# A Fourier-mixing and channel-mixing kernel: in the first batch, a butterfly two steps further down VectorE's queue, two PSUM evacuations exchanged between engines, and fewer filler products

## The chip, the cores and the metric

The kernel runs on one core of a Trainium2 chip. The metric is the time of one execution on the device, in microseconds (us). Times given for a kernel are medians of several runs; a profile is one further look at a single execution, and its span is the time from that execution's first recorded instruction to its last.

## The reference

For `x` of shape (8, 3072, 256) the kernel computes the real part of a two-dimensional Fourier transform of each batch, and then a channel mix with a look at the row before:

```python
X = fft(fft(x, axis=1), axis=2).real
X_prev = rows of X shifted down by one, first row zero
xk = mu_k * X + (1 - mu_k) * X_prev
xr = mu_r * X + (1 - mu_r) * X_prev
k  = relu(xk @ w_k)            # 256 -> 1024
v  = (k * k) @ w_v             # 1024 -> 256
out = sigmoid(xr @ w_r) * v
```

## The kernel before

**Tiling.** The transform over 3072 rows is split as 48 x 64. Per batch it goes through three product stages on TensorE (PE), each followed by a copy out of PSUM (an *evacuation*):

- Stage A (`a_sum`, L384, and `a_item`, L372) transforms over the 48. Batch 0 and the first half of batch 1 use `a_sum`, which takes `x` as it was loaded and does the sum over the two halves of the columns inside PE with two products per row group. The others use `a_item`, which takes sums and differences made beforehand on VectorE (DVE) by `butterfly` (L115). A butterfly `(b, h, e)` reads the loaded half `h` of batch `b` and makes the sum (`e` = 0) or the difference (`e` = 1).
- Stage B (`d_item`, L407) transforms over the 256 columns and writes `g_all`.
- Stage C (`c_item`, L418) transforms over the 64; its evacuation writes the tile `pq`. The arguments are a first slice and a number of slices of 64 columns.

From `pq`, DVE makes the spectrum and the mixed inputs: `halves` (L438), `diff` (L445), and `mix` or `mix2` (L479, L483), which run `scaled` (L453) and `mixed` (L466) and write the tiles `x00` to `x11`.

**The channel mix** works on 48 chunks of 512 rows, 6 per batch (two mirrored sets m of three). Each chunk has four pieces. `k_piece` (L502) does four products of 512 columns on PE and a relu on ScalarE (ACT). `square` (L511) squares two pieces on DVE. `r_item` (L515) does eight products of 256 columns, once per chunk, and a sigmoid on ACT. `v_tile` (L527) does eight products of 256 columns, and `v_out` (L538) multiplies two v tiles by the sigmoid on DVE and stores them.

**What sets the order.** The order is written out by hand and pinned per engine (`pin_order`, L85): each engine does its instructions in the order in which the program emits them. The main loop (L688) goes through 192 steps and 5 more. In step s it emits `k_piece` s, then the items of kind "x" that are due in s (stages A, B, C and `r_item`, in the order in which `at` was called), then `v_tile` of step s - 5, then the items of kind "w" (all DVE work and the loads of x), then, when s - 5 is odd, `v_out`, and in odd steps `square`. `at(step, function, ...)` (L596) enters an item; the lines that matter here are L609 to L660. An evacuation belongs to its stage's item, so it is emitted with the "x" items, on ACT unless the item's last argument is "V", which puts it on DVE (`evac`, L363).

**Buffers.** Product groups of the k and r products and of the stages A, B and C write to PSUM tiles `psW`, of which there are three, used in turn (`ps_w`, L74). So a group can begin only when the group three places before it has been evacuated. The v products and the fillers use `psV`, two in turn. There are two buffers for the loaded halves of x (`xh`, L109), so the load of half `(2, 1)` waits until the butterflies of `(1, 1)` have read it.

**Ahead of the loop** the first two stage C groups of batch 0 are done, DVE makes the first 512 columns of `x00`, and the first k products are split in two halves of 256 columns. `keep_busy(n)` (L138) emits n products of 512 columns of zeros that nobody reads: fillers for TensorE.

The steps that the change touches belong to the first batch. There `r_item` of the third chunk is due in step 12; it reads `x10`, whose last third is written by `mix2(0, 1, 0, 16, 24)`, due in step 10. `a_sum(1, 0, 4)` and `a_sum(1, 0, 8)` are due in step 5, `c_item(0, 17, 8)` in step 3.

Of the kernel before, what the change touches and what calls it, by code (L numbers as in the profile page):

```python
# [35 lines left out]
def kernel(  # L36
# [40 lines left out]
    def ps_v():  # L77
        return ps_slot("V", 2, 512)
# [34 lines left out]
    V = nc.vector  # L113
# [24 lines left out]
    def keep_busy(n):  # L138

        ps = ps_v()  # L140
        for _ in range(n):
            nc.tensor.matmul(out=ps[:, 0:512], lhsT=zeros[:, 0:P], rhs=zeros, start=True, stop=True)
# [346 lines left out]
    def k_products(c, ds, lo=0, hi=512):  # L489
        b, m, i = c  # L490
        xk = x_t[b, 0, m]
        if lo == 0:
            st["k", ds] = ps_w()
        for hs in range(2):
            fc = 2 * ds + hs
            for a in range(2):
                nc.tensor.matmul(out=st["k", ds][:, 512 * hs + lo:512 * hs + hi],  # L497
                                 lhsT=wk_sb[m][a][:, 128 * fc:128 * fc + 128],
                                 rhs=xk[:, a, 512 * i + lo:512 * i + hi],
                                 start=(a == 0), stop=(a == 1))  # L500
# [95 lines left out]
    def at(step, f, *args):  # L596
        work.setdefault((step, "x" if f in (a_item, a_sum, d_item, c_item, r_item) else "w"),
                        []).append((f, args))
# [10 lines left out]
    keep_busy(4)  # L609
    k_products(chunks[0], 0, 0, 256)  # L610
    k_products(chunks[0], 1, 0, 256)
    keep_busy(4)
    for n, c in enumerate(chunks):
        at(4 * n + 4, r_item, c)


    at(0, m_swap, NS1, NSL)
# [6 lines left out]
    at(1, mix2, 0, 0, 0, 8, 16)  # L624
    at(2, d_item, 0, 5)
    at(2, a_sum, 1, 0, 0)
    at(3, c_item, 0, 17, 8)
    at(3, butterfly, 1, 1, 0)
    at(4, halves, 0, 17, 25)
    at(4, diff, 0, 16, 24)  # L630
    at(5, a_sum, 1, 0, 4)
    at(5, a_sum, 1, 0, 8, "V")
    at(5, mix2, 0, 0, 0, 16, 24)
    at(6, a_sum, 1, 0, 12)
    at(6, c_item, 0, 25, 2)
    at(6, load_xh, 2, 0)
    at(6, mix2, 0, 1, 0, 8, 16)
    at(6, butterfly, 1, 1, 1)
    at(7, halves, 0, 25, 27)
    at(7, diff, 0, 24, 26)  # L640
    at(7, mirrored_mu)
# [92 lines left out]
```

## Time and profile before

| | us |
|---|---|
| median of 5 runs | 466.0 |
| lowest and highest of the 5 | 464.26, 466.8 |
| the profiled execution, its own time | 464.91 |
| its span | 463.1 |
| PE busy in the span | 452.6 (98%) |
| DVE busy | 357.6 (77%) |
| ACT busy | 357.6 (77%) |
| GpSimd busy | 34.9 (8%) |

The time of an execution is a little longer than its span: 464.91 beside 463.1.

How to read the lines. A line of a timeline gives the start in us from the beginning of the span, the duration of the merged instructions, the engine (PE for products, PEld for weight loads, DVE, ACT, POOL for GpSimd), the line of the kernel, the operation, the tile written and the tile read, the shape, how many instructions were merged (x8), and in brackets how long the engine sat idle before it and what ended the wait. Durations of successive instructions overlap by a little, so the distance between starts says how long an engine is really held. The ends of products are modelled, so for PE too the starts are what counts. A line of the chain that ended last gives start, length and what; it is followed back from the last instruction of the kernel, at each point to what released it.

The profile by stages (busy time of each engine between two moments) reads: from 24 to 32 us PE 7.27, DVE 7.09, ACT 7.86 of 8; from 32 to 52 us PE 19.46, DVE 19.51, ACT 15.79 of 20; from 52 to 456 us PE 404.00, DVE 310.06, ACT 319.52 of 404. The batches overlap: while the channel mix of one batch runs, the stages of the next are woven in.

### The profile page before, as it was taken

The page shows a single profiled execution, that of the slowest core. Times are in us where ns is not written, and L with a number is a line of the kernel's source. Part 1 is how long each engine was busy: PE and PEld are TensorE (multiplying, and loading weights), DVE is VectorE, ACT ScalarE, POOL GpSimd, SP SyncE. Part 2 cuts the span into 40 slices and gives each one's busy share as a digit, 9 for nine tenths or more (in the row PEclk, how much of TensorE's full clock was granted, in tenths as well). Part 3 has the DMA queues.
Part 4 walks back from the last instruction along what each step waited for, and adds up shares of the span by engine and source line. Part 5 has one row for each costly group of instructions (what it writes and reads, how often), then busy time and mean ns, then how long its engine had stood idle before and what let it go on. Part 6 is the DMA issues. An engine that isn't in the chain of part 4 may idle for free.

```text
span 463.1 us, 10098 instructions
## 1 busy us (share of the span) xinstructions
PE 452.6 (98%) x4266; PEld 332.3 (72%) x4266; DVE 357.6 (77%) x495; ACT 357.6 (77%) x390; POOL 34.9 (8%) x67
## 2 busy tenths in 40 slices
PE   6899999999999999999999999999999999999996
PEld 3667777777777777777777777777777777776665
DVE  7799968986788777978588776888679854898443
ACT  3897898788778887888778888878877888666662
POOL 8821000001000000000000000000000000000000
PEclk9999999999999999999999999999999999999999
DMA  7896451625612373224722265212222222223323
GB/s 120 146 169 106 113 126 47 138 68 115 137 47 70 58 146 95 69 58 92 156 63 62 54 137 115 69 47 69 49 68 55 60 65 51 70 53 80 74 64 96
DMA packets 32721, 40.24 MB, mean 87 GB/s; under 512 B 4228, under 2 KB 30340, under 8 KB 31332
## 3 DMA queue, kind: packets, MB, share of 16 engines
q1 hardware_dynamic: 27828, 25.05, 21.7%
q0 software_dynamic: 4688, 14.42, 18.4%
q8 instruction: 33, 0.54, 0.5%
q10 hardware_dynamic: 160, 0.13, 0.1%
q14 instruction: 12, 0.10, 0.1%
HBM read 28.84 MB, written 25.17 MB: 117 GB/s over the span
## 4 chain that ended last, share of the span: by engine, by line
PE 87%; DMA 4%; DVE 4%; POOL 2%; issue 1%; SPq 0%; POOLq 0%; DVEq 0%
PE psV L534 34%; PE psW L497 33%; PE psW L520 9%; PE psW L403 4%; DMA xh<-in_x_dram 4%; PE psW L430 4%; PE psW L379 4%; POOL xh L106 1%; DVE k L513 1%; DVE x L475 1%; DVE t L462 1%; DMA out_dram<-o 1%; DVE eo L119 1%; DVE o L543 1%; POOL mu_f L325 0%
## 5 line engine op out<-in xcount | busy, mean ns | idle before, releaser
L507 ACT ACTIVATE rl<-psW 128x1024 f16<-128x1024 f32 x192 | 196.7, 1025 | 87.6 <-PE psW L497 87.6
L497 PE MATMUL psW<-x,wk 128*128 128x512 f16 (+1 forms) x776 | 197.4, 377 | 1.3 <-DVE x L475 1.1
L534 PE MATMUL psV<-wv_sb,k 128*128 128x256 f16 x1536 | 198.6, 272 | 0.0
L513 DVE TENSOR_TENSOR k<-rl 128x2048 f16<-128x2048 f16 x96 | 117.4, 1223 | 65.0 <-ACT rl L507 64.3
L534 PEld LDWEIGHTS <-k 128*128 128x128 f16 x1536 | 143.6, 98 | 20.3
L497 PEld LDWEIGHTS <-wk 128*128 128x128 f16 x776 | 75.7, 98 | 51.7 <-issue 2.2
L543 DVE SCALAR_TENSOR_TENSOR o<-psV,r 128x512 f32<-128x512 f32 (+1 forms) x97 | 66.2, 683 | 29.0 <-PE psV L534 27.0
L475 DVE TENSOR_TENSOR x<-y,t 128x1536 f16<-128x1536 f16 (+2 forms) x74 | 62.9, 851 | 2.5
L367 ACT ACTIVATE a<-psW 128x768 f16<-128x768 f32 x61 | 49.2, 809 | 4.5 <-PE psW L393 4.4
L520 PE MATMUL psW<-wr,x 128*128 128x256 f16 x384 | 49.9, 273 | 0.4 <-DVE x L475 0.4
L525 ACT ACTIVATE r<-psW 128x1024 f16<-128x1024 f32 x48 | 49.0, 1021 | 1.3 <-PE psW L520 1.3
L520 PEld LDWEIGHTS <-x 128*128 128x128 f16 x384 | 37.5, 98 | 15.2 <-DVE x L475 1.0
L367 ACT ACTIVATE g_all<-psW 128x1024 f16<-128x1024 f32 (+1 forms) x47 | 47.7, 1021 | 0.0
L106 POOL DMA_DIRECT2D xh<-in_x_dram x38 | 19.7, 524 | 241.4 <-DVE eo L119 230.2
L403 PEld LDWEIGHTS <-a 128*128 128x128 f16 x384 | 25.0, 98 | 10.5 <-issue 0.4
L119 DVE TENSOR_TENSOR eo<-xh 96x2048 f16<-96x2048 f16 x26 | 31.6, 1214 | 0.6 <-DMA xh<-in_x_dram 0.6
L379 PEld LDWEIGHTS <-eo 96*128 96x128 f16 x416 | 23.4, 97 | 11.6
L367 ACT ACTIVATE pq<-psW 128x896 f16<-128x896 f32 (+5 forms) x33 | 28.6, 869 | 0.3 <-PE psW L430 0.3
L403 PE MATMUL psW<-w_eo,a 128*128 128x128 f16 x376 | 28.3, 219 | 0.3 <-ACT pq L367 0.3
L430 PEld LDWEIGHTS <-g_all 128*128 128x128 f16 x648 | 23.3, 98 | 6.9 <-ACT g_all L367 0.2
L379 PE MATMUL psW<-w_pm,eo 96*128 96x96 f16 x416 | 26.3, 206 | 0.0
L430 PE MATMUL psW<-m,g_all 128*128 128x64 f16 x648 | 24.5, 193 | 0.1
(89 smaller groups left out, 148.3 us busy)
## 6 DMA issues: line engine op xcount, KB each, us to landing
out_dram<-o SPq DMA_DIRECT2D x190, 128.0 KB, 2.4
xh<-in_x_dram POOLq DMA_DIRECT2D x28, 384.0 KB, 6.2
xh<-in_x_dram POOLq DMA_DIRECT2D x6, 192.0 KB, 6.2
wv_sb<-in_moe_w_v_dram POOLq DMA_DIRECT2D x1, 512.0 KB, 8.6
xh<-in_x_dram POOLq DMA_DIRECT2D x4, 96.0 KB, 7.2
out_dram<-o ACTq DMA_DIRECT2D x2, 64.0 KB, 2.0
out_dram<-o SPq DMA_DIRECT2D x2, 64.0 KB, 2.0
wk<-in_moe_w_k_dram,row_i POOLq DMA_INDIRECT x4, 4.8
```

What stands on the lines that cost most here:

```text
L367: nc.scalar.activation(out=out_ap, in_=in_ap, func=AF.Copy)
L379: nc.tensor.matmul(out=ps[:, 128 * i:128 * i + 96], lhsT=eo[:, 8 * j + i, e, :], rhs=w_pm[0:96, 0], start=True, stop=True)
L403: nc.tensor.matmul(out=_v(ps, 256 * i + 64 * (1 - e), [(128, 2), (1, 64)]), lhsT=a_t[b][:, e, 2 * u:2 * u + 2, :], rhs=w_eo[:, e, :], star ...
L430: nc.tensor.matmul(out=ps[:, o + 64 * i:o + 64 * i + 64], lhsT=g_all[:, u, col:col + 128], rhs=m[:, sl], start=first, stop=last)
L475: V.tensor_tensor(out=dst, in0=_v(y_t[b], 64 * (NSL * a + lo + 3 * m), [(1, n)]), in1=_v(x_t["t", a], 64 * lo, [(1, n)]), op=ALU.subtract ...
L497: nc.tensor.matmul(out=st["k", ds][:, 512 * hs + lo:512 * hs + hi], lhsT=wk_sb[m][a][:, 128 * fc:128 * fc + 128], rhs=xk[:, a, 512 * i + l ...
L507: nc.scalar.activation(out=st["rl"][:, 2 * ds:2 * ds + 2], in_=st["k", ds].rearrange("p (f t) -> p f t", f=2), func=AF.Relu, bias=0.0, sca ...
L513: V.tensor_tensor(out=k2_t[c][:, 2 * ds - 2:2 * ds + 2], in0=r, in1=r, op=ALU.mult)
L520: nc.tensor.matmul(out=ps[:, 256 * tb:256 * tb + 256], lhsT=x_t[b, 1, m][:, a, 512 * i + 128 * tb: 512 * i + 128 * tb + 128], rhs=wr_sb[m] ...
L525: nc.scalar.activation(out=st["r", c], in_=ps, func=AF.Sigmoid)
L534: nc.tensor.matmul(out=st["v"][:, 256 * h:256 * h + 256], lhsT=k2_t[c][:, fc, 128 * tb:128 * tb + 128], rhs=wv_sb[:, fc], start=(fc == 0), ...
L543: V.scalar_tensor_tensor(out=o.rearrange("p a b -> p (a b)")[:, 0:256 * n], in0=st["v"][:, 0:256 * n], scalar=16.0, in1=st["r", c][:, 256 ...
```

## The change

All of it lies in the first batch:

- The second group of fillers in front of the loop has 2 products in place of 4.
- `r_item` of the third chunk is due in step 13 in place of 12.
- The evacuation of `c_item(0, 17, 8)` (stage C, step 3) goes to DVE. That of `a_sum(1, 0, 8)` (stage A, step 5) goes from DVE to ACT.
- The butterfly `(1, 1, 0)` is due in step 5 in place of 3. In step 5 it is the first "w" item, since the call of `at` stands where it stood, ahead of `mix2(0, 0, 0, 16, 24)`.
- The butterfly `(1, 1, 1)` is due in step 7 in place of 6, ahead of `halves(0, 25, 27)`.

```diff
@@ -609,9 +609,9 @@
     keep_busy(4)
     k_products(chunks[0], 0, 0, 256)
     k_products(chunks[0], 1, 0, 256)
-    keep_busy(4)
+    keep_busy(2)
     for n, c in enumerate(chunks):
-        at(4 * n + 4, r_item, c)
+        at(4 * n + (5 if n == 2 else 4), r_item, c)
 
 
     at(0, m_swap, NS1, NSL)
@@ -624,18 +624,18 @@
     at(1, mix2, 0, 0, 0, 8, 16)
     at(2, d_item, 0, 5)
     at(2, a_sum, 1, 0, 0)
-    at(3, c_item, 0, 17, 8)
-    at(3, butterfly, 1, 1, 0)
+    at(3, c_item, 0, 17, 8, "V")
+    at(5, butterfly, 1, 1, 0)
     at(4, halves, 0, 17, 25)
     at(4, diff, 0, 16, 24)
     at(5, a_sum, 1, 0, 4)
-    at(5, a_sum, 1, 0, 8, "V")
+    at(5, a_sum, 1, 0, 8)
     at(5, mix2, 0, 0, 0, 16, 24)
     at(6, a_sum, 1, 0, 12)
     at(6, c_item, 0, 25, 2)
     at(6, load_xh, 2, 0)
     at(6, mix2, 0, 1, 0, 8, 16)
-    at(6, butterfly, 1, 1, 1)
+    at(7, butterfly, 1, 1, 1)
     at(7, halves, 0, 25, 27)
     at(7, diff, 0, 24, 26)
     at(7, mirrored_mu)
```

## The prediction, made before the changed kernel had run

> **What bounds the kernel now.** I read three views in this order. First the busy time by stages: from 52 us to 456 us TensorE (PE) is busy in all 404.00 of 404 us, so nothing that happens there can be shortened by reordering; whatever this change is worth must be a PE gap before 52 us. Only the start of the main loop is open.
>
> Second, the chain that ended last (start, length, what). It shows whom PE waits for last:
>
> ```profile
> 21.61 10.41 DMA xh<-in_x_dram
> ...
> 32.11 1.22 DVE eo L119
> 33.33 1.14 DVE k L513
> ...
> 50.35 0.44 DVE x L475
> 50.79 0.05 issue
> 50.84 0.94 PE psW L520 x7
> 51.78 0.45 PE psW L403 x8
> ```
>
> A load of x (second half of batch 1) lands at 32.02; VectorE (DVE) had stood still for it and starts the butterfly at 32.11. From there DVE works without a gap to 50.79, and there PE takes over. So a late landing at 32 us is paid once, at 50.84, by the first r product group that needs DVE's last mix.
>
> Third, the PE timeline around that point and around the fillers:
>
> ```profile
> 22.29 1.03 PE L142 MATMUL psV<-zeros 128*128 128x512 f16 x4
> 23.16 0.27 PE L497 MATMUL psW<-x,wk 128*128 128x256 f16 x1
> 23.61 0.93 PE L497 MATMUL psW<-x,wk 128*128 128x256 f16 x7 [0.18 <-DVE x L475]
> ...
> 49.20 1.03 PE L497 MATMUL psW<-x,wk 128*128 128x512 f16 x4
> 50.11 0.28 PE L520 MATMUL psW<-wr,x 128*128 128x256 f16 x1
> 50.84 0.94 PE L520 MATMUL psW<-wr,x 128*128 128x256 f16 x7 [0.44 <-DVE x L475]
> 51.61 0.61 PE L403 MATMUL psW<-w_eo,a 128*128 128x128 f16 x8
> ```
>
> One r product starts at 50.11 and the next only at 50.84. Eight of them take 0.87 us elsewhere (0.109 each), so PE lost 50.84 - 50.22 = **0.62 us**. Between 30.5 and 50.1 the starts of groups follow one another at their own lengths, except at step 5.
>
> Step 5 is ruled by ScalarE (ACT), which has no gap from 24.14 to 35.7:
>
> ```profile
> 31.17 1.11 ACT L367 ACTIVATE pq<-psW 128x1024 f16<-128x1024 f32 x1
> 32.07 1.12 ACT L507 ACTIVATE rl<-psW 128x1024 f16<-128x1024 f32 x1
> 32.98 1.14 ACT L525 ACTIVATE r<-psW 128x1024 f16<-128x1024 f32 x1
> ```
>
> There are three psW slots, used in turn, so a PE group waits until the group three places earlier has been emptied. The second of the two a_sum groups of step 5 waits for the sigmoid that ends at 34.12: the two groups take 33.25 to 34.82 = 1.57 us, where one alone (36.56 to 37.22) takes 0.66, so 0.25 us are lost. Waits of 0.04 to 0.05 stand before k5, k4's successor r and the first a_sum.
>
> **The change, part by part.**
>
> *r products of the third chunk, step 12 to 13.* PE then does in step 12: k products 0.87, stage B 0.45 (8 products), v 0.87; in step 13: k 0.87 and only then r. Counted from 49.20 (later 49.30, see below), r starts at 52.40. DVE's last mix ends at 50.79 now, about 50.34 then. Slack 2 us: the 0.62 us go. What is late next? ACT gets four copies in step 13 (relu, sigmoid, two of stage B) at a pitch of 0.92, 3.7 us, against 3.5 us of PE. I followed the slots: the tightest is the first stage C group of batch 1 in step 14, whose slot comes free at 56.41 where PE arrives at 56.40; all others have 0.1 to 0.6 us. The v_out that multiplies by this sigmoid is in step 14 at 59.48 on DVE, 5 us after it. So **-0.62**; bounds -0.62 and -0.3 (three waits of 0.1 by the ACT pitch).
>
> *Exchange of evacuations.* Stage C's copy of 128x1024 leaves ACT (0.90 of pitch at 31.17) for DVE. No DVE copy of that size is in the trace; the three that are, 384, 512 and 768 columns, take 0.557, 0.69 and 0.954, that is 1.03 ns a column, so 1024 would take 0.954 + 0.265 = 1.22 us, and hold DVE 1.14 (a copy's successor starts 0.08 before its end). Nearest rows as bounds: ACT's 1.07 for the same shape and DVE's 1.36 for 128x1152 int32. I take 1.22. In front of it on DVE is the square that starts at 30.32 and holds DVE until 31.46. So the slot comes free at 31.46 + 1.22 = 32.68 where ACT frees it at 32.28: the k products of step 5 start at 32.73 in place of 32.33, **+0.40**. On the other hand ACT now does relu 4 and the sigmoid earlier (the sigmoid ends near 33.6, since it follows its products, done at 32.45), so the 0.25 wait and one of 0.05 vanish: k5 32.73, a_sum 33.60 and 34.26, v at 34.92 where it is 34.82 now. Net **+0.10**. Bounds: -0.34, if the copy frees its slot by 32.29 (0.25 + 0.05 + 0.04), and +0.25 with the 1.36 row. The a_sum copy that goes from DVE (0.87 of occupancy) to ACT (0.69) follows the relu that ends at 34.8 and is done by 36.3; its slot is wanted at 37.3. ACT has 1.03 us idle there now, so it costs nothing; without that cover it would be 0.69.
>
> *Butterflies down the queue.* The first, 1.14 of occupancy, goes from step 3 to step 5, behind the square, halves and diff; the second from step 6 to 7, behind one v_out. DVE's sum from 31.54: -0.57 idle, -0.87, +1.14, with the overlaps about -0.45; everything from step 5 on is that much earlier. Consumers of the butterflies: stage A of step 7, PE at 39.2, the result there at 36.4 (now 33.3); step 9, PE at 44.3, the result at 42.1. Behind them: the squares that v needs are earlier, not later. The load into the buffer that the second butterfly frees is issued on GpSimd at 42.4 in place of 42.18; it is read by DVE after 57. So **0** on the path in this execution. But the landing may now slip to about 35.1 before any engine waits, where now every 0.1 us of slip is 0.1 us at 50.84.
>
> *Two fillers less.* 4 x 0.216 become 2 x 0.216: PE is free at 22.72 in place of 23.16. The half-group behind needs DVE's x, whose two parts end at 23.03 and 23.56. So the first product starts 0.08 earlier, and the other seven again at 23.61: **0**. Cover: the wait for DVE. What it can cost is the clock. At the start eleven fillers take 4.87 us, 0.443 each, twice the 0.216 of later: PE begins at half rate. Between 20.14 and 23.61 PE now idles 0.51 + 0.77 + 0.34 = 1.62 of 3.47 us, then 2.06, but the longest single gap stays 0.77, and the unbroken gap from 9.07 to 10.52 left the next 16 products at the same 1.48 us as those before it. So I take 0; the other end is in the rival below.
> [...]
>
> **Sum.** -0.62 + 0.10 = -0.52 us on the profiled execution: 464.91 becomes 464.4 (span 463.1 to 462.6, 1.8 outside it). The median of the five runs is 466.0, 1.09 above the profiled one. If that excess arises before 21 us, the change leaves it: 465.5. If it is a later landing of x at 32 us, which DVE hands on to PE in full, it goes: 464.4. The trace has one execution and can't tell; I take the middle, **464.9 us**, with 464.4 to 465.5 around it.
>
> **Rivals.**
> 1. *More is won.* The excess is all due to the landing, and the stage C copy on DVE is as quick as its lower bound: -0.62 - 0.34 = -0.96, 463.95 on the profiled execution, say 463.9. For it: the one load on the chain of waits is this one, in flight for 10.4 us while the DMA engines are full. Against: the extrapolated 1.22.
> 2. *The wait moves, and nothing is won.* The copy takes 1.36 (+0.25) and ACT makes PE wait in steps 13 and 14 (0.3 of the 0.62 given back): -0.07, 465.9 from the median. For it: a slot with no margin at 56.4. Against: ACT has the same pitch there as now.
> 3. *Slower: the clock falls* near 23.5 because PE is idle 59% of 3.47 us where it was 47%. The only half-rate stretch in the trace is 4.87 us long. Such a stretch does half its work, 2.43 us lost, of which the PE gaps between 23.6 and 28.5 (0.16 + 0.47 + 0.46 = 1.09) absorb at most 1.09. With -0.62 for r that is +0.7 to +1.8: 466.7 to 467.8, middle 467.3. It decides as soon as a stretch of over 3.5 us (1.09 + 0.62, doubled) is at half rate. Against: the 1.45 us gap that did nothing.
>
> **How the numbers follow.** Forecast 0.55, rival 1 0.18, rival 2 0.15, rival 3 0.12. A measurement of this kernel can tell about 0.3% (1.4 us) from no change; the bounds are 464.6 and 467.4. The forecast's own range lies on both sides of 464.6: 0.20 faster, 0.35 same. Rival 1 is faster (0.18), rival 2 same (0.15), rival 3 slower 0.10 and same 0.02. So faster 0.38, same 0.52, slower 0.10. The range goes from below rival 1 to the mild end of rival 3: 463.5 to 466.7.
>
> **What would show it.** Right: no gap inside the r products of the third chunk, which stand behind k of step 13; DVE without idle time at 31.5 and the butterfly at about 35.1; the stage C copy at 31.46 for 1.2 us; k of step 5 at 32.7 and v at 34.9; products of 256 columns at 0.109 from 23.6 on; PE without gaps from 36 us on. Wrong: group times near double after 23.6 (the clock), a copy well off 1.2, waits on ACT between 53 and 57, or the same 0.6 us in front of another group in steps 12 to 16. If the span falls by 0.5 and the median by as little, the excess was not the landing.

## The result, and the profile after

| | before | after |
|---|---|---|
| median, us (64 and 38 runs) | 465.23 | 464.31 |
| lowest, highest | 464.16, 467.42 | 462.98, 465.88 |
| profiled execution, own time and span | 464.91, 463.1 | 464.33, 462.6 |

The ratio of the times is 0.9975, with a 95% interval of 0.9968 to 0.9982: the changed kernel is 0.25% (1.16 us, 0.84 to 1.49) faster. That is a gain, and smaller than 0.3%. The two profiled executions differ by 0.58 us. The spread differs too. Of the 64 runs before, 41 took over 465 us, of the 38 after only 3. Of the runs after, 14 are under the lowest of before, and 18 lie between 464.20 and 464.45.

The PE timeline of the changed kernel, around the fillers and at the r products of the third chunk:

```profile
22.22 0.59 PE L142 MATMUL psV<-zeros 128*128 128x512 f16 x2
23.02 0.27 PE L497 MATMUL psW<-x,wk 128*128 128x256 f16 x1 [0.20 <-DVE x L475]
23.55 0.92 PE L497 MATMUL psW<-x,wk 128*128 128x256 f16 x7 [0.26 <-DVE x L475]
...
49.23 1.03 PE L497 MATMUL psW<-x,wk 128*128 128x512 f16 x4
50.09 0.61 PE L403 MATMUL psW<-w_eo,a 128*128 128x128 f16 x8
50.53 1.04 PE L534 MATMUL psV<-wv_sb,k 128*128 128x256 f16 x8
51.41 1.03 PE L497 MATMUL psW<-x,wk 128*128 128x512 f16 x4
52.27 1.04 PE L520 MATMUL psW<-wr,x 128*128 128x256 f16 x8
53.15 1.06 PE L403 MATMUL psW<-w_eo,a 128*128 128x128 f16 x16
```

The eight r products now stand as one group of 0.88 us between starts; the hole of 0.62 us is gone. At the fillers PE waits a little longer for DVE and goes on at the same place (23.55 beside 23.61).

DVE in the kernel before, where it waits for the load, then in the changed kernel, and PE at step 5 of the changed kernel:

```profile
32.11 1.22 DVE L119 TENSOR_TENSOR eo<-xh 96x2048 f16<-96x2048 f16 x1 [0.57 <-DMA xh<-in_x_dram]
```

```profile
31.39 1.22 DVE L365 CAST pq<-psW 128x1024 f16<-128x1024 f32 x1
32.53 1.21 DVE L513 TENSOR_TENSOR k<-rl 128x2048 f16<-128x2048 f16 x1
...
35.05 1.21 DVE L119 TENSOR_TENSOR eo<-xh 96x2048 f16<-96x2048 f16 x1
```

```profile
32.66 1.02 PE L497 MATMUL psW<-x,wk 128*128 128x512 f16 x4 [0.28 <-DVE pq L365]
33.52 1.49 PE L393 MATMUL psW<-w_pm,xh 96*128 96x192 f16 x16
34.84 1.04 PE L534 MATMUL psV<-wv_sb,k 128*128 128x256 f16 x8
```

DVE has no idle time for the load any more; the stage C copy took 1.22 us. The k products of step 5 wait for that copy, the a_sum pair after them takes 1.32 in place of 1.57, and v comes at 34.84, where it came at 34.82. The chain that ended last now goes from DVE to PE at that copy, at 32.66, and not at the r products at 50.84.

### The profile page after: what moved, and what is told of

Same layout as the page of the kernel before. It is cut to its first block, busy times and chain, and to the rows that moved or that the text cites. A ratio compares the mean times of both kernels' runs of the same rounds, so it can differ in the third digit from the quotient of the medians.

```text
span 462.6 us, 10095 instructions
## 1 busy us (share of the span) xinstructions
PE 451.2 (98%) x4264; PEld 332.0 (72%) x4264; DVE 358.0 (77%) x495; ACT 357.6 (77%) x390; POOL 35.1 (8%) x67
## 4 chain that ended last, share of the span: by engine, by line
PE 92%; DVE 3%; DMA 2%; POOL 1%; issue 0%; ACT 0%; SPq 0%; POOLq 0%; DVEq 0%
PE psV L534 36%; PE psW L497 35%; PE psW L520 9%; PE psW L403 4%; PE psW L379 4%; PE psW L430 4%; DMA xh<-in_x_dram 2%; POOL xh L106 1%; DVE t L462 1%; DVE x L475 1%; DMA out_dram<-o 1%; PE psW L393 0%; DVE y L442 0%; DVE d L450 0%; DVE pq L365 0%
## 5 line engine op out<-in xcount | busy, mean ns | idle before, releaser
L367 ACT ACTIVATE pq<-psW 128x896 f16<-128x896 f32 (+5 forms) x32 | 27.4, 861 | 0.3 <-PE psW L430 0.3
```

Source lines behind the costliest of these rows:

```text
L367: nc.scalar.activation(out=out_ap, in_=in_ap, func=AF.Copy)
```

## The experiments

Theories, as they stood after this profile. **L**, the landing: the load of x (1, 1) lands near 32 us, at a somewhat different time in each execution; DVE waits for it and PE waits for DVE at the r products, so the kernel before pays each lateness in full. **R** and **Q**: what was taken away is the wait of the r products, a matter of queue order, and the spread of the runs comes from the start. **X**: the gain is the lighter queue of ACT. **F**: fillers are paid in executions in which PE comes late.

The kernels ran in three groups of four; each group has its own runs of the kernel before, and ratios are against those.

| kernel | median, us | before in its group | ratio (95%) | span of its profile |
|---|---|---|---|---|
| late_before | 467.93 | 466.67 | 1.0021 (1.0007 to 1.0035) | 466.4 |
| late_after | 466.00 | 466.67 | 0.9978 (0.9964 to 0.9992) | 464.2 |
| early_before | 467.26 | 466.67 | 1.0008 (0.9996 to 1.0020) | 465.3 |
| r_only | 466.92 | 466.67 | 1.0004 (0.9996 to 1.0013) | 465.2 |
| no_r | 464.53 | 465.70 | 0.9982 (0.9968 to 0.9997) | 461.8 |
| no_x | 464.32 | 465.70 | 0.9967 (0.9952 to 0.9982) | 461.4 |
| fill4 | 464.35 | 465.70 | 0.9971 (0.9958 to 0.9984) | 462.5 |
| no_bf | 464.36 | 465.70 | 0.9973 (0.9960 to 0.9986) | 462.4 |
| r_only_2 | 466.73 | 466.74 | 0.9996 (0.9985 to 1.0007) | 465.6 |
| x_only | 466.83 | 466.74 | 0.9999 (0.9987 to 1.0010) | 464.8 |
| bf_only | 468.24 | 466.74 | 1.0034 (1.0019 to 1.0049) | 466.4 |
| split | 466.77 | 466.74 | 0.9997 (0.9986 to 1.0008) | 465.7 |

In the first and the third group the kernel before itself is 1.0 us above the second. The kernel before was not profiled in these groups, nor was the whole change without a further edit among their kernels. Every profile there shows a late start with the same kind of wait, told under the first group. The profiled executions with a halved clock in their middle (late_before, early_before, r_only, r_only_2, bf_only, split) have a mean granted clock of 0.991 to 0.996, the others 0.998 to 1.000; the runs are compared on that below.

### The load later or earlier

late_before is the kernel before, late_after the changed kernel, both with:

```diff
         nc.gpsimd.dma_start(out=wv_sb, in_=moe_w_v.rearrange("(fc p) v -> p fc v", p=128))
-        load_xh(1, 1)
         for a in range(2):
             gather(wk_sb[1][a], moe_w_k, 2 + a)
+        load_xh(1, 1)
```

> The kernel before, with the load of x (1, 1) issued behind the two gathers of the second w_k, about 2.6 us later. Theory L (the gain is the landing of this load, which DVE hands on to the r products): DVE waits longer ahead of the butterfly of step 3, by as much as the landing is later, some 1 to 2 us from its 32.0; the butterfly and the square behind it start later by that, and the v products of step 5 or the r products of the third chunk wait longer by the same; time 1 to 2 us above the kernel before, 466.2 to 467.2. Theory Q (the gain is the order of r and the lighter ACT queue; the spread of the runs arises elsewhere): at most 0.3 us slower, 465.5.

> The changed kernel with the same later load. Theory L: the landing stays ahead of 35.05, where DVE now comes to the butterfly, so no wait of DVE for a load and the time of the changed kernel, 464.3 (0.2% under the kernel before). Theory Q: the same as for the kernel before with the later load, that is 0 to 0.3 us above the changed kernel. If the landing falls behind 35.05, slower by the difference.

early_before is the kernel before with:

```diff
+        load_xh(1, 1)
         nc.gpsimd.dma_start(out=wv_sb, in_=moe_w_v.rearrange("(fc p) v -> p fc v", p=128))
-        load_xh(1, 1)
```

> The kernel before, with the load of x (1, 1) issued ahead of that of w_v, about 1 us earlier. Theory L: DVE's wait of 0.57 us at 31.5 goes, and with it most of the 0.62 us ahead of the r products of the third chunk (0.05 to 0.15 stay); the runs lie closer together; 464.3 to 464.6, nearly the whole gain of the change with none of its edits. Theory Q: the r products wait as before, 465.2.

The signs came as L has them for the later load: 0.21% slower before, no loss after. For the earlier load L failed: nearly the whole gain was expected, and the ratio is 1.0008. But the profiles don't let either count as proof. DVE in late_before, then in early_before:

```profile
35.06 1.21 DVE L119 TENSOR_TENSOR eo<-xh 96x2048 f16<-96x2048 f16 x1
```

```profile
32.79 1.22 DVE L119 TENSOR_TENSOR eo<-xh 96x2048 f16<-96x2048 f16 x1
```

In neither does DVE wait for the load: it comes to the butterfly at 35.06 and 32.79, because everything before had become late. The last line of the load's semaphore events is at 34.2 in late_before and 34.7 in late_after, 2.2 and 2.6 us later than the 32.02 of the kernel before, and still ahead of DVE. So the expected cost could not appear in these executions. The halved clock, told next, adds to the times of some runs but does not explain the order: among the runs with a mean granted clock of 0.998 or more, six of late_before have a median of 467.53, eleven of the kernel before 466.46 and eleven of late_after 465.99. That fits L: the later load costs the kernel before about 1 us and leaves the changed kernel ahead; but no such run of late_before was profiled, and what it waits for is not shown.

In late_before, r_only, early_before, r_only_2, bf_only and split TensorE's granted clock is 0.50 for one or two stretches of 3.41 us. The stages of r_only_2 around one of them, and one stage of x_only (of the same group, without a halving):

```profile
core 0: us, PE busy (x) PEld busy (x) DVE busy (x) ACT busy (x) POOL busy (x), PEclk, DMA share, GB/s
26.75:30.16 3.41, 1.54 (x19) 1.07 (x17) 1.52 (x5) 2.25 (x4) 0.75 (x1) 1.00 1.07 208
30.16:33.57 3.41, 3.40 (x21) 2.24 (x21) 3.31 (x7) 2.71 (x4) 0.00 (x0) 0.50 1.06 192
```

```profile
26.36:29.77 3.41, 1.81 (x20) 1.23 (x19) 1.50 (x5) 2.23 (x3) 1.09 (x1) 1.00 1.10 210
29.77:33.18 3.41, 3.00 (x41) 1.98 (x39) 3.27 (x7) 3.41 (x5) 0.00 (x0) 1.00 1.04 188
```

In r_only_2 PE was busy for 1.54 of 3.41 us, and in the next 3.41 us the clock was 0.50; in x_only it was busy for 1.81, and the clock stayed 1.00. All eight halvings in these profiles, leaving out those behind the last products, follow a stretch with 1.15 to 1.61 us of PE (34 to 47%). In no_r a stretch has 1.75 (4.54 to 7.95, 51%) and none follows: the mean clock of that execution is 1.000. The longest single wait does not sort them: it is 1.49 us in split's stretch, which was followed by a halving, and 1.60 us in x_only's, which was not.

What emptied those stretches is a wait of 1.5 to 2.6 us that has no work behind it, PE in r_only_2:

```profile
27.07 0.61 PE L403 MATMUL psW<-w_eo,a 128*128 128x128 f16 x8
29.25 0.61 PE L403 MATMUL psW<-w_eo,a 128*128 128x128 f16 x8 [1.57 <-ACT pq L367]
30.17 1.44 PE L393 MATMUL psW<-w_pm,xh 96*128 96x192 f16 x8 [0.31 <-ACT rl L507]
```

PE waits for ACT's copy, and ACT is idle too, waiting for PE, whose groups are recorded as done: in early_before the stage C group starts at 23.98 and the last group ahead of the wait at 25.51 (0.61 long); ACT's copy of the stage C group begins at 27.62, after 2.39 us without work, and PE goes on at 28.70, after 2.57. Similar waits of PE, of 2.45, 2.08 and 2.38 us, stand between 14 and 18 us in late_before, r_only and bf_only. The first halving in late_before and bf_only, at 7.4 us, is another case; it follows a wait of 2.0 us for DVE at the start of stage A. What held the copies back is not shown. What the waits do is: PE comes to the k products of step 3 at 32.80 in late_before, where it is 28.89 in the kernel before, and DVE to the butterfly at 35.06 for 31.54, when the load has landed.

### Single parts

r_only and r_only_2 are the same kernel: the kernel before with

```diff
-        at(4 * n + 4, r_item, c)
+        at(4 * n + (5 if n == 2 else 4), r_item, c)
```

> The kernel before with one edit: the r products of the third chunk in step 13. Both theories: the wait of 0.62 us goes, since DVE's last mix ends near 50.8 and the products start near 52.3; no new wait between 52 and 57. Theory L: a landing up to 1.5 us later is covered too, unless the v products of step 5 meet the square late (their margin is 0.35 us), so most of the excess goes: 464.3 to 464.6. Theory Q: only the wait goes, 464.6, and the spread of the runs stays that of the kernel before.

> The kernel before with the r products of the third chunk in step 13 alone, once more, beside the other single parts. Theory L (the landing near 32 to 32.7 us, handed on by DVE, is what the kernel before is paced by; any edit that keeps DVE's lateness from PE brings the gain): the wait ahead of r goes, the slack behind it is 1.5 us; the v products of step 5 meet the square late only if the landing is behind 32.6. Ratio 0.9975 to 0.9985 on a chip where the first run of this kernel's long idle times of ACT between 14 and 28 us don't occur. Rival: the single edit brings nothing (ratio 1.000, as in the first run), since PE then waits for the square in step 5 instead.

x_only is the kernel before with `"V"` added to `c_item(0, 17, 8)` and taken from `a_sum(1, 0, 8)`:

```diff
-    at(3, c_item, 0, 17, 8)
+    at(3, c_item, 0, 17, 8, "V")
...
-    at(5, a_sum, 1, 0, 8, "V")
+    at(5, a_sum, 1, 0, 8)
```

> The kernel before with the two evacuations exchanged and nothing else. Theory L: DVE does the stage C copy while the load is still under way, comes to the butterfly at 32.5, and is 0.45 us earlier from there on when the landing is before that; of the 0.62 us ahead of the r products of the third chunk 0.15 to 0.2 stay; the k products of step 5 wait 0.4 for DVE, the second a_sum no longer for the sigmoid. Ratio 0.9985 to 0.999. Theory X (ACT's queue): 0.998.

bf_only is the kernel before with the butterflies alone:

```diff
-    at(3, butterfly, 1, 1, 0)
+    at(5, butterfly, 1, 1, 0)
...
-    at(6, butterfly, 1, 1, 1)
+    at(7, butterfly, 1, 1, 1)
```

> The kernel before with the two butterflies in steps 5 and 7 and nothing else. No wait of DVE for the load; but DVE stands idle for about 1 us ahead of the a_sum copy of step 5, which PE finishes at 35.0, and the butterfly comes behind that. DVE's last mix ends 0.2 to 0.3 us later than in the profile of the kernel before, and the wait ahead of r grows from 0.62 to about 0.9. Theory L: ratio 1.000, between 0.999 and 1.0005: what the landing no longer costs, the hole costs. Theory that the butterfly's place alone is the gain: 0.998.

Neither r alone nor the exchange alone gained anything (1.0004, 0.9996, 0.9999). But these runs are of the groups with the late start; DVE waits for the load in none of the profiles, so L has nothing to win there. Nor has R: late_before and early_before have r of the third chunk in step 12, and their eight r products already run in one piece (53.98 to 54.86 and 52.90 to 53.77). What the single edits do in an undisturbed execution is not shown. In r_only_2 there is no hole at the r products either. In x_only there is one, 52.10 to 52.53:

```profile
52.10 0.27 PE L520 MATMUL psW<-wr,x 128*128 128x256 f16 x1
52.53 0.94 PE L520 MATMUL psW<-wr,x 128*128 128x256 f16 x7
```

With 0.109 for the first product it is 0.32 us, more than the 0.15 to 0.2 expected. bf_only is clearly slower, 0.34%, and more than expected; its profile has the hole of DVE and what it costs at the r products:

```profile
37.88 0.96 DVE L365 CAST a<-psW 128x768 f16<-128x768 f32 x1 [1.00 <-PE psW L393]
```

```profile
52.14 1.03 PE L497 MATMUL psW<-x,wk 128*128 128x512 f16 x4
53.38 0.28 PE L520 MATMUL psW<-wr,x 128*128 128x256 f16 x1 [0.21 <-DVE x L475]
54.10 0.94 PE L520 MATMUL psW<-wr,x 128*128 128x256 f16 x7 [0.44 <-DVE x L475]
```

From 52.14 + 0.87 = 53.01 the first product waits 0.37 us and the second 0.61, together 0.98; 0.9 was expected. That is about two thirds of the 1.5 us by which the median is longer; the profile also has two halved stretches, and only three of its eleven runs have a mean clock of 0.998 or more (median 467.72, the kernel before 466.58), so the rest is not sorted out. The butterflies' move alone is a loss, as far as this group can tell: it needs the exchange to fill DVE's time, or r out of its way, as in no_r and no_x below.

### The change without one of its parts

Each is the changed kernel with one part as before: no_r has r of the third chunk in step 12, no_x the evacuations on their old engines, no_bf the butterflies in steps 3 and 6, fill4 four fillers (the diffs above, read backwards; for fill4 `keep_busy(2)` is `keep_busy(4)`).

> The changed kernel with the r products of the third chunk back in step 12. Theory R (the wait ahead of them is what the change took away): in an execution without other delays PE reaches them at 50.1 and DVE's last mix ends at 50.35, so 0.1 to 0.3 us of the wait come back; 0.05% above the changed kernel, ratio to the kernel before 0.998. Theory L (the landing): the butterfly is out of the way of the landing already, so the same 0.998. If ACT's queue counts (theory X), as good as the changed kernel.

> The changed kernel with the two evacuations on their old engines (stage C on ACT, the a_sum of step 5 on DVE). Theories R and L: the k products of step 5 no longer wait for DVE (0.44 us), but the second a_sum of step 5 waits for the sigmoid (0.25), and DVE stands idle for about 1 us until that a_sum is done; PE comes to the v products of step 5 at 34.8 as before; same time as the changed kernel, ratio 0.9975. Theory X (the gain lies in the lighter ACT queue): 0.4 to 0.9 us above the changed kernel, ratio 0.9985 to 0.9995.

> The changed kernel with four fillers in the second group, as before. Theories R, L and X: the same time as the changed kernel, ratio 0.9975, since the k products wait for DVE either way. Theory F (in executions where PE comes late to this place, x is there already and every filler is paid): up to 0.43 us above the changed kernel, ratio 0.998 to 0.9985; on the other hand no execution in which the clock halves near 23.5.

> The changed kernel with the two butterflies back in steps 3 and 6; stage C's copy on DVE stays ahead of the first. Theory L: the butterfly starts at 32.5 behind that copy, so a landing up to 0.5 us later than 32.0 is covered and a later one is passed on to DVE only, while the r products of step 13 keep 1.5 us of slack: same time as the changed kernel when the landing is before 33, ratio 0.9975; if landings are often later, the square behind it comes late for the v products of step 5 and the time rises by 0.3 us or more. Theories R, X, F: ratio 0.9975.

All four are as fast as the whole change (0.9975, measured against other runs of the kernel before) within what this group can tell (0.9967 to 0.9982, intervals of 0.0013 to 0.0015 to each side). So no single part is needed for a gain, and X falls: without the exchange the ratio is 0.9967. F is not seen: with four fillers 0.9971, though the interval reaches the 0.998 that F would give. Nor is the gain a matter of the clock: among the runs with a mean granted clock of 0.998 or more, 28 of the kernel before have a median of 465.51, and no_r, no_x, fill4 and no_bf have 464.52, 464.32, 464.35 and 464.36.

The profiles say why. no_r keeps a small rest of the hole; its r group takes 50.27 - 49.19 = 1.08 us between starts, 0.21 more than 0.87, where 0.1 to 0.3 was expected:

```profile
49.19 1.25 PE L520 MATMUL psW<-wr,x 128*128 128x256 f16 x8
50.27 0.61 PE L403 MATMUL psW<-w_eo,a 128*128 128x128 f16 x8
```

no_x has the expected hole on DVE ahead of the a_sum copy, and its butterfly after it:

```profile
33.86 0.96 DVE L365 CAST a<-psW 128x768 f16<-128x768 f32 x1 [0.91 <-PE psW L393]
34.73 1.21 DVE L119 TENSOR_TENSOR eo<-xh 96x2048 f16<-96x2048 f16 x1
```

It costs nothing, since r is in step 13 and has the slack. no_bf is the one that shows the landing, DVE and then PE:

```profile
30.08 1.22 DVE L365 CAST pq<-psW 128x1024 f16<-128x1024 f32 x1
32.68 1.22 DVE L119 TENSOR_TENSOR eo<-xh 96x2048 f16<-96x2048 f16 x1 [1.39 <-DMA xh<-in_x_dram]
33.83 1.22 DVE L513 TENSOR_TENSOR k<-rl 128x2048 f16<-128x2048 f16 x1
```

```profile
33.53 0.60 PE L534 MATMUL psV<-wv_sb,k 128*128 128x256 f16 x4
35.10 0.61 PE L534 MATMUL psV<-wv_sb,k 128*128 128x256 f16 x4 [0.96 <-DVE k L513]
```

This execution started 1.3 us quicker than that of the changed kernel (its v products would have run on from 33.53, where the changed kernel has 34.84). The load landed at 32.59. DVE waited 1.39 us for it with the butterfly in step 3, the square behind the butterfly was late, and PE stood 1.14 us between the fourth and the fifth v product (33.53 + 0.43 = 33.96 to 35.10). Nearly all of the quick start was lost; the span is 462.4. no_x, with an equally quick start (PE at 33.66) and the butterfly behind the load, lost nothing: span 461.4. So a butterfly in step 3 ties the kernel to the landing from below, and this is the mechanism of L in a profile.

### One step further

split is the changed kernel with the stage C copy of step 3 in two halves, each on its own engine:

```diff
+        if eng == "AV":
+            for h, e in enumerate("AV"):
+                evac(pq[:, h, s0:s0 + n, :], _v(ps, 512 * h, [(64, n), (1, 64)]), e)
...
-    at(3, c_item, 0, 17, 8, "V")
+    at(3, c_item, 0, 17, 8, "AV")
```

> The changed kernel with the stage C copy of step 3 split by its two halves, one on ACT and one on DVE, 128x512 each. DVE's half takes 0.69 us and frees the slot near 32.2, so the wait of the k products of step 5 (0.28 as the profile counts it, 0.44 between starts) goes, and the sigmoid comes in time for the second a_sum. All theories: v of step 5 at about 34.4 in place of 34.84, ratio to the kernel before 0.9965, 0.4 us under the changed kernel. If ACT's relu behind the half copy becomes late, 0.2 us under it.

No wait of the k products of step 5 is left, and the a_sum pair takes 1.32 us. But r_only_2, without any exchange, has the same after the same halved stretch (36.62 to 37.95), so this says nothing on the split. But the two halves did not run side by side, as the expectation had it; DVE's half stood until ACT's half, from 34.32 to 34.91, was done:

```profile
34.95 0.69 DVE L365 CAST pq<-psW 128x512 f16<-128x512 f32 x1 [1.47 <-ACT pq L367]
```

Its ratio of 0.9997 tells one thing more: split has all edits of the change, and in this group it gains nothing. So the gain of the whole change may itself be absent in executions with such a start. No version is shown to be better than the change; no_x, the change without the exchange, is as good within the intervals.

## Why the prediction was right

- **What bounds the kernel**: right. PE is busy in all 404.00 us from 52 to 456 after as before, and all that changed lies ahead of that.
- **r products**: -0.62 expected, and the hole went. Behind them PE is 0.65 ahead (53.15 beside 53.80), and from step 14 on 0.61 (the next r group at 61.45, before at 62.06); the last store is issued 0.60 earlier (456.30 beside 456.90). The tight place in step 14 was rightly named: 55.77 to 56.31 is 0.54 for a group of 0.45; the prediction had put 0 there.
- **Exchange**: copy of 1.22 expected, 1.22 measured; it started at 31.39 for 31.46. v expected 0.10 later, measured 0.02 in an execution that was 0.07 ahead when it came there (30.43 beside 30.50): 0.09.
- **Butterflies**: DVE's last mix expected at 50.34, measured 49.92 + 0.42 = 50.34; the butterfly expected at 35.1, measured 35.05. The agreement to the hundredth is partly luck: DVE was 0.06 ahead when it came there (square at 30.26 beside 30.32), so the change itself moved the last mix by about 0.39 and not by the 0.45 of the prediction, whose terms do not add up to it (0.57 + 0.87 - 1.14 is 0.30; with the idle time counted between starts, 0.65, it is 0.38).
- **Fillers**: 0 expected, and fill4 agrees. The reason given was only half right. The prediction argued from the longest single gap; in the runs it is the share of a 3.41 us stretch that goes with the halvings. Between 20.00 and 23.55 PE is busy for 2.08 of 3.55 us after (59%), between 20.14 and 23.61 for 2.33 of 3.47 before (67%): both over the 51% of no_r's stretch, after which the clock stayed up; the 3.41 us stretches as they fell in the profile after have 2.50 (17.87 to 21.28) and 2.77 us (21.28 to 24.69). The distance to the 47% after which it fell in split is smaller than the prediction thought.
- **The sum**: 0.52 expected on the profiled execution, 0.58 measured from one profiled execution to the other.
- **The excess of the median**: the prediction could not tell whether it came from the start or from the landing, and took half of it, for 1.1 in all (466.0 to 464.9); measured 0.92 between the medians and 1.16 by the ratio. That this fits is partly luck. The 1.09 was the excess of a median of five runs; over 64 runs the median is 465.23 and the excess 0.32, less than the half that was taken. So 464.9 was 0.6 too high, and 464.31 lies just below the 464.4 to 465.5 around it. On the cause there is now more to say. In the six profiles with an undisturbed start (before, after, no_r, no_x, no_bf, fill4) the load lands at 32.02, 31.82, 33.50, 32.75, 32.59 and 32.55: 32.5 in the mean, 0.5 later than in the profiled execution of before, over a range of 1.7 us. If the kernel before hands that on in full, 0.58 and 0.5 make 1.08. Five more profiles, with a late start but the load issued at the same place (r_only, r_only_2, x_only, bf_only, split), have 32.05, 32.55, 31.98, 31.41 and 32.73; with them the mean is 32.4, and the sum 0.92. That a larger part of the runs after gathers at one time fits as well. It is still an inference: no run of the kernel before with a known late landing and an undisturbed start was profiled.

**Rival 1** (more is won, 463.9 on the profiled execution) failed on the copy, which was as slow as extrapolated; on the landing it is nearer than the forecast, if that inference holds. **Rival 2**: the wait did not move, but for the 0.09 of step 14. **Rival 3**: the clock did not fall in the profile of the changed kernel (1.00 up to 456 us). That PE's idle share could bring it down was an assumption when it was written; in six profiles of the experiments it did fall, to 0.50, after stretches with PE idle for 53 to 66%. The rival tied the fall to this edit, while in the runs it came after other waits. A halved stretch cost PE about 1.1 us by step 5: r_only_2 and x_only stand level at 29.25 and 29.31, and v of step 5 is at 37.95 and 36.86; the spans of the two, which differ in their edits too, are 0.8 apart. The estimate of up to 2.4 us from a stretch of 4.87 was too long; the stretches are 3.41.

**Still open**: what each edit is worth alone in an undisturbed execution, whether the change gains anything in executions with a late start, and what holds back ACT's copies of PE's groups in the first and third group.

## What to carry to other kernels

An instruction that waits for a load, in a queue that works without a gap behind it, makes the landing time of that load the kernel's pace, where another engine meets the end of that queue without slack (in no_bf 1.39 us of DVE's wait for the load became 1.14 us of PE's). Put it behind work that needs no load, and give what reads the end of that queue some slack too; when several edits do this, each can look worthless when it is undone alone. And compare the places at which two executions start the stage in question before crediting an edit: a late start can hide the very wait that it removes (in early_before and late_before DVE came to the butterfly at 32.79 and 35.06 and did not wait, in the kernel before it waited 0.57 us).

## What the runs showed of the hardware that was not expected

- In these runs the granted clock went with PE's share of a stretch and not with the longest gap: after the eight stretches of 3.41 us with PE busy 34 to 47% it was 0.50 for the next 3.41 us, after those of no_r and x_only with 51 and 53% it stayed 1.00. The longest single wait did not decide it (1.49 us with a halving in split, 1.60 us without in x_only). One halved stretch held PE back by about 1.1 us at step 5 (r_only_2 beside x_only).
- The load of x (1, 1), issued by GpSimd while the DMA engines were full (share 1.10 from 21 to 32 us in the kernel before, 1.09 up to the landing in the changed one), landed between 31.41 (bf_only) and 33.50 (no_r) in the eleven profiles that issue it at the same place, though the issue times (20.99 to 21.48) differ by 0.5 us only.
- In the first and third group ACT's copies of finished groups came late: in early_before 3.6 us after the recorded start of a stage C group (23.98 to 27.62), with ACT idle for 2.39 us before the copy and DVE for 1.84 us until it was done; in the kernel before the copy of that group came 1.6 us after its start (24.38 to 25.96), with no idle time of ACT.
